# Phases before exponentials, and W1 by three powers: reordering the kernel-generation groups of an S4D block

## The chip, the cores and the metric

The kernel runs on one core of a Trainium2 chip. The metric is the device time of one execution in microseconds (us). The engines of a core run side by side, each with its own instruction queue worked off in order: PE (matrix products; its weight loads are listed as PEld), DVE (vector), ACT (activation functions and copies), POOL (vector work and DMA issue), SP (DMA issue). Semaphores order them.

## The reference

One transformer-like block over 2048 tokens of width 576, all in fp32: an S4D long convolution and a feed-forward layer, each behind a layer norm with scale and shift, and with a gated residual.

```python
# S4D: a long convolution per channel d, N = 128 complex states
A = -exp(log_A_real) + 1j * A_imag;  dt = exp(log_dt);  C = (C_real + 1j * C_imag) * dt
P = exp((A * dt)[:, :, None] * pos)              # pos = 0 .. 2047
K = 2 * einsum("dn,dnl->dl", C, P).real
y = irfft(rfft(u, 4096) * rfft(K, 4096))[:2048] + u * D_skip
# the block
sa, ca, ga, sb, cb, gb = split(silu(c) @ w_mod, 6)
h = layernorm(x) * (1 + ca) + sa
x = x + ga * S4D(h)
h = layernorm(x) * (1 + cb) + sb
x = x + gb * (relu(h @ w1) @ w2)                 # 576 -> 4608 -> 576
```

## The kernel before

**Stages.** The tokens are four blocks of 512. First the convolution kernel `K` is generated for block 0 of positions, in six groups of 96 channels (`KGen.first`, L324). Then block 0 is convolved (`Body.conv(0)`, L937) by short Fourier transforms on PE with butterflies on DVE, and normed. From there the feed-forward layer (`ffn`, L1264) runs over 4 x 36 steps, with fp32 split in a high and a low part, so 14 products a half step. Its steps are interleaved with the rest of the kernel values (`KGen.rest`) and the convolutions of blocks 1 to 3.

**One kernel group.** Position l is written as 16 coarse values of step 32 (`W1`) times 32 fine ones (`W2`); PE multiplies them over the 128 states (`products`, 96 pairs of small products for each half `u` of a group), and ACT copies the result to `ke` (`rows`, L351), which is stored to DRAM (`kd`) after every third group, and later loaded as `kt`. For each group:

- `turns` (L192): PE spreads the phases into PSUM (`ph`), ACT rounds them to an integer (`k`), DVE takes the difference (`f`, the phase within a turn). Three pieces: odd, even, powers.
- `exps` (L182): PE spreads the rates into PSUM (`ph`), ACT takes the exponential (`E`). Five pieces, E0 to E4.
- `sines` (L333): ACT takes sines and cosines of `f`, DVE and POOL multiply them by `E` into `W2`; `powers` (L262) makes the powers z^32 to z^1024 of which four stay in PSUM (`Z`), two are stored (`zs`, `Zd`); `moduli` multiplies the four by `E`.
- `doubling` (L283): `W1` grows from 1 value to 2, 4, 8, 16, each time by one power of `Z`: two products into `t` and `T`, and a difference and a sum. The first two take both halves of the group at once, the last two half by half; the last has its differences and sums on POOL.

In iteration g the loop finishes `W1` of group g, makes `E` and `f` of group g+1, copies `ke` of group g-1, then multiplies group g (first half `a` at once, second half `late` in portions in the next iteration, by `some`) and takes the sines of g+1.

**What sets the order.** All of `KGen` issues through helpers (`act` L58, `v` L61, `stt` L64, `pool` L67, `matmul` L70) that keep each engine's instructions in the order in which the program issues them. So the order written in `first` (L324) is the order on each queue. In the profile these helpers' lines stand for all instructions of `KGen`. `Kept` (L41, L47 in the profile) does the same elsewhere. The PSUM tiles of phases, rates and sines share one pair of buffers, taken in turn:

```python
def banks(self, name):
    return self.ph.tile([P, 2, 512], F32, tag="ph", bufs=2, name=name)
```

`ph` takes half of PSUM; `Z` (two banks), `T` and the result `kps` take the other half.

**Beside the groups.** `setup` (L82) prepares phases and rates of all channels, in portions; `mod` and `mod_late` (L736) make the modulation vectors; `early` (L607) loads x's first block, takes its statistics with the groups and makes `h`, in portions that the loop draws. `skip` adds `D_skip` to the first row of a loaded `kt`. In `conv(0)`, `spec_U` and `spec_K` make the spectra of x and `K` (`Ud`, `Rd` in DRAM, from POOL's queue).

## Time and profile before

| | |
|---|---|
| median of 3 runs | 1326.09 us (1322.65 to 1332.2) |
| profiled execution, its time and span | 1328.0 us, 1326.2 us |
| mean granted PE clock | 0.943 |
| busy in the span: PE, DVE, ACT, POOL | 1212.6, 895.2, 494.3, 160.3 us |
| kernel groups | about 35 to 160 us |
| first feed-forward product | 223.56 us |

How to read the rows that follow: a row of the timeline begins with the start and the duration in us, then the engine, the line in the kernel, the operation, the tiles written and read, and the shape. Instructions of a kind that follow one another are merged into a row (x4), whose duration runs from the first to the last. In brackets stands how long the engine was idle before, and what ended that ("issue": nothing that the profile shows). ACT, DVE and PE are the engines themselves, SPq and POOLq their DMA issues. On the page, part 2 cuts the span into 40 slices, with the busy share in tenths and the PE clock that the throttle granted in tenths of full speed.

### The profile page before, as it was taken

To read this page: it belongs to the slowest core of one execution; us is meant where nothing else is said; L and a number is where in the kernel's file an instruction comes from. 1 tells how busy PE (TensorE), PEld (TensorE's weight loads), DVE (VectorE), ACT (ScalarE), POOL (GpSimd) and SP (SyncE) were. 2 spreads that over 40 slices of the span, in tenths; PEclk is the share of its full clock that TensorE was granted. 3 is DMA by queue.
4 is the path that set the end of the run, shared out by engine and by line. 5 is a ranking of instruction groups with operands and counts; after the bars stand their busy time and mean duration, and the time that the engine had idled before them with its cause. 6 is when DMAs were issued, how large, how long until landed. Compare 5 with 4: busy or idle time off the path is not lost.

```text
span 1326.2 us, 25994 instructions
## 1 busy us (share of the span) xinstructions
PE 1212.6 (91%) x10720; PEld 960.7 (72%) x10720; DVE 895.2 (67%) x1324; ACT 494.3 (37%) x863; POOL 160.3 (12%) x256
## 2 busy tenths in 40 slices
PE   4566676899989999999999999999999999999998
PEld 3344554677767787777777887887888888888886
DVE  5989988999986999689468994457996222111112
ACT  5677623222223422622243225433323353223231
POOL 0756511011000100100001000100000000000000
PEclk9556777999989999999999999999999999999999
DMA  8567882889878967799779995867996667666652
GB/s 273 210 235 294 300 314 80 345 298 333 311 259 302 342 223 278 247 403 343 262 270 339 351 340 159 285 205 285 346 395 189 173 177 230 195 202 191 200 178 70
DMA packets 122635, 345.85 MB, mean 261 GB/s; under 512 B 23916, under 2 KB 24212, under 8 KB 111764
## 3 DMA queue, kind: packets, MB, share of 16 engines
q1 hardware_dynamic: 105940, 228.14, 51.8%
q0 software_dynamic: 16064, 114.67, 23.0%
q8 instruction: 84, 1.38, 0.4%
q10 hardware_dynamic: 512, 1.38, 0.3%
q14 instruction: 35, 0.29, 0.1%
HBM read 262.73 MB, written 81.40 MB: 259 GB/s over the span
## 4 chain that ended last, share of the span: by engine, by line
PE 70%; DVE 17%; DMA 6%; issue 4%; ACT 2%; POOL 1%; SPq 0%; ACTq 0%; DVEq 0%; POOLq 0%
PE hps L1330 28%; PE acc L1356 28%; PE ps_f L850 5%; DMA L1d<-w 3%; PE kps L71 2%; PE ph L71 2%; DVE W1r L484 2%; DVE T L482 2%; PE ps_i L1057 2%; PE kps L517 1%; DVE w L1300 1%; DMA x<-in_x_dram 1%; DVE W1r L486 1%; DVE W1r L488 1%; DVE w L1312 1%
## 5 line engine op out<-in xcount | busy, mean ns | idle before, releaser
L1330 PE MATMUL hps<-xh,w 128*128 128x512 f32 x1152 | 395.7, 404 | 0.7 <-ACT xh L47 0.7
L1356 PE MATMUL acc<-w,hh 128*128 128x512 f32 x1136 | 362.1, 401 | 3.7 <-ACT hh L1335 3.5
L1336 DVE SCALAR_TENSOR_TENSOR hl<-hps,hh 128x512 fp32r<-128x512 f32 x144 | 99.4, 690 | 309.2 <-ACT hh L1335 308.5
L1330 PEld LDWEIGHTS hps<-xh,w 128*128 128x128 f32 x1152 | 219.0, 191 | 48.9 <-ACT xh L47 1.3
L1356 PEld LDWEIGHTS acc<-w,hh 128*128 128x128 f32 x1136 | 212.4, 188 | 50.3 <-ACT hh L1335 4.4
L1330 PE MATMUL hps<-xl,w 128*128 128x512 f32 x576 | 228.0, 397 | 0.1
L1356 PE MATMUL acc<-w,hl 128*128 128x512 f32 x568 | 219.8, 399 | 1.5 <-DVE hl L1336 1.5
L1335 ACT ACTIVATE hh<-hps 128x512 fp32r<-128x512 f32 x144 | 86.0, 597 | 329.9 <-PE hps L1330 325.2
L1305 ACT ACTIVATE w<-r 128x576 fp32r<-128x576 f32 x141 | 96.7, 686 | 225.3 <-PE acc L1356 224.9
L1330 PEld LDWEIGHTS hps<-xl,w 128*128 128x128 f32 x576 | 109.2, 190 | 23.5 <-DVE xl L47 0.6
L1356 PEld LDWEIGHTS acc<-w,hl 128*128 128x128 f32 x568 | 106.1, 188 | 25.4 <-DVE hl L1336 3.3
L1295 ACT ACTIVATE w<-r 128x640 fp32r<-128x640 f32 x140 | 102.5, 732 | 51.2 <-DMA L1d<-w 50.5
L1330 PE MATMUL hps<-xs,w 128*128 128x512 f32 x288 | 98.7, 412 | 0.0
L71 PE MATMUL kps<-W,W 128*32 128x16 f32 x2304 | 39.4, 210 | 45.8 <-POOL W L68 28.1
L1036 DVE TENSOR_TENSOR Y<-Y,T 128x1152 f32<-128x1152 f32 x60 | 79.5, 1353 | 0.0
L71 PEld LDWEIGHTS kps<-W,W 128*32 128x32 f32 x2304 | 34.6, 142 | 59.5 <-POOL W L68 31.2
L851 ACT ACTIVATE Z<-ps_f 128x288 f32<-128x288 f32 x120 | 48.9, 409 | 71.1 <-PE ps_f L850 69.3
L517 PEld LDWEIGHTS kps<-W1r,W2r 128*32 128x32 f32 x3456 | 45.1, 113 | 38.6 <-issue 19.2
L517 PE MATMUL kps<-W1r,W2r 128*32 128x48 f32 (+2 forms) x3456 | 52.4, 202 | 15.5 <-ACT ker L527 10.8
L1330 PEld LDWEIGHTS hps<-xs,w 128*128 128x128 f32 x288 | 53.8, 190 | 11.3
L1356 PE MATMUL acc<-hh,w 128*128 128x512 f32 x142 | 56.9, 401 | 0.0
L1356 PE MATMUL acc<-hl,w 128*128 128x512 f32 x142 | 56.1, 395 | 0.0
(249 smaller groups left out, 1547.1 us busy)
## 6 DMA issues: line engine op xcount, KB each, us to landing
r<-in_w_dram SPq DMA_DIRECT2D x144, 320.0 KB, 6.0
r<-in_w_dram SPq DMA_DIRECT2D x144, 288.0 KB, 3.7
w<-L1d SPq DMA_DIRECT2D x108, 320.0 KB, 4.2
w<-L2d SPq DMA_DIRECT2D x108, 288.0 KB, 2.6
W2r<-W2d POOLq DMA_DIRECT2D x18, 1536.0 KB, 9.0
W2d<-W SPq DMA_DIRECT2D x12, 1536.0 KB, 8.7
Ua<-Ud POOLq DMA_DIRECT2D x15, 1152.0 KB, 9.3
W<-W1d POOLq DMA_DIRECT2D x18, 768.0 KB, 9.5
```

The source lines that it names most:

```text
L71: self.tc.keep_in_program_order(self.nc.tensor.matmul(*args, **kw))
L482: v(T, X, zi, op=ALU.mult)
L517: nc.tensor.matmul(ps[32 * dd : 32 * dd + 32, q, :], W2[:, r, ch], W1[:, r, ch], start=(r == 0), stop=(r == 1),)
L850: nc.tensor.matmul(o, fc[:, n2, c, :], src(n2), start=True, stop=True)
L851: ev = nc.scalar.activation(Z[:, n2, c], ps[:, :PC], AF.Copy)
L1036: v(y, y, T, op=op or ALU.add)
L1295: copy(g - 1)(w1[g][:, 0], r1[g], AF.Copy)
L1305: copy(g)(w[:, 0:D], r2[g], AF.Copy)
L1330: nc.tensor.matmul(ps, a, x, start=(i == 0), stop=(i == 13))
L1335: nc.scalar.activation(hh, ps, AF.Relu)
L1336: nc.vector.scalar_tensor_tensor(hl, ps, 0.0, hh, op0=ALU.max, op1=ALU.subtract)
L1356: nc.tensor.matmul(acc[i], a, x, start=(f == 0 and seen[i] == 1), stop=(f == NF - 1 and seen[i] == (3 if i < 4 else 2)),)
```

## The change

- *Order in a group.* The phases of the next group (`turns`) are issued ahead of its exponentials, in portions between the first two doublings; the five exponentials come after the first half of the new wide products. The statistics of x's tiles come after all of these.
- *W1 by three powers.* A seventh power, z^384, is made. The doublings for 8 and 16 values go. Instead `quarters` multiplies the first 4 values by z^128, z^256 and z^384 at once: for the real and for the imaginary part two products on DVE (96 x 3 x 4 = 1152 elements each) and one sum on POOL. `Z` holds five powers.
- *D_skip* is added by POOL to `ke` before it is stored, no longer to `kt` (`skip` goes); its array is laid out on the host as an added input layout.
- *x's spectra* of block 0, and that of `K`, are stored after the transform of the second `kt` has been issued, all three from POOL's queue in program order.
- *First phases early.* `setup` has one more portion: the phases of channels past the first third are prepared ahead of the silu of `c`, the rates after it.
- *mod_late* transposes each row one portion later; `zs` has a layout in which each half is stored contiguously.

```diff
@@ -32,7 +32,8 @@
 TURN_LO = 1.0 / TWO_PI - TURN_HI
-POWERS = (32, 64, 128, 256, 512, 1024)
+POWERS = (32, 64, 128, 256, 384, 512, 1024)
+NP = len(POWERS) - 2
 SLOTS = (*range(1, 32, 2), *range(0, 32, 2), *POWERS)
@@ -139,6 +140,7 @@
             turn(h)
+        yield
         self.act(lar[:, 4:], lar[:, 4:], AF.Exp)
@@ -182,7 +184,7 @@
         E = self.E[g] = []
-        for s0, n in ((0, 8), (8, 8), (16, 8), (24, 8), (32, 6)):
+        for s0, n in ((0, 8), (8, 8), (16, 8), (24, 8), (32, NS - 32)):
             e = self.pt.tile([P, 2, 8 * H], F32, tag="E", bufs=8, name=f"E_{g}")
@@ -192,7 +194,7 @@
         F = self.F[g] = []
-        for s0, n in ((0, 8), (17, 8), (32, 6)):
+        for s0, n in ((0, 8), (17, 8), (32, NS - 32)):
             k = self.pt.tile([P, 2, 8 * H], I32, tag="k", bufs=3, name=f"k_{g}")
@@ -261,50 +263,63 @@
-        Z = self.ps.tile([P, 2, 512], F32, tag="Z", name=f"Zp_{g}")[:, :, 0 : 4 * G]
+        Z = self.ps.tile([P, 2, 512], F32, tag="Z", name=f"Zp_{g}")[:, :, 0 : NP * G]
         Z = Z.rearrange("p r (i c) -> p r i c", c=G)
-        zs = self.pc.tile([P, 2, 2, G], F32, tag="zs", bufs=2, name=f"zs_{g}")
+        zs = self.pc.tile([P, 2, 2, 2, H], F32, tag="zs", bufs=2, name=f"zs_{g}")
         by_u = lambda x: x.rearrange("p i (u c) -> p u i c", u=2)
         c = self.abs(f)
-        self.act(by_u(Z[:, 1]), f[:, :, 0:4], AF.Sin, scale=-TWO_PI)
-        self.act(by_u(zs[:, :, 1]), f[:, :, 4:6], AF.Sin, scale=-TWO_PI)
-        self.cos(by_u(Z[:, 0]), c[:, :, 0:4])
-        self.cos(by_u(zs[:, :, 0]), c[:, :, 4:6])
+        self.act(by_u(Z[:, 1]), f[:, :, 0:NP], AF.Sin, scale=-TWO_PI)
+        self.act(zs[:, :, :, 1], f[:, :, NP:], AF.Sin, scale=-TWO_PI)
+        self.cos(by_u(Z[:, 0]), c[:, :, 0:NP])
+        self.cos(zs[:, :, :, 0], c[:, :, NP:])
         for r in (1, 0):
-            self.pool(by_u(zs[:, :, r]), by_u(zs[:, :, r]), e[:, :, 4:6], op=ALU.mult)
+            self.pool(zs[:, :, :, r], zs[:, :, :, r], e[:, :, NP:], op=ALU.mult)
         self.Z[g] = Z, zs
...
             for r in (1, 0):
-                self.v(by_u(Z[:, r]), by_u(Z[:, r]), e[:, :, 0:4], ALU.mult)
+                self.v(by_u(Z[:, r]), by_u(Z[:, r]), e[:, :, 0:NP], ALU.mult)
...
-    def doubling(self, g, i, u):
-
-        v, p = self.v, self.pool
-        Z = self.Z[g][0]
-        m, n = 1 << i, (u.stop - u.start) * H
-        W1 = self.W1[g][:, :, u].rearrange("p r u c a -> p r (u c) a")
+    def doubling(self, g, i):
+
+        v = self.v
+        m = 1 << i
+        W1 = self.W1[g].rearrange("p r u c a -> p r (u c) a")
         X, out = W1[:, :, :, 0:m], W1[:, :, :, m : 2 * m]
         zr, zi = (
-            Z[:, r, i, u.start * H : u.stop * H].unsqueeze(1).unsqueeze(3)
-            .broadcast_to([P, 2, n, m])
+            self.Z[g][0][:, r, i].unsqueeze(1).unsqueeze(3).broadcast_to([P, 2, G, m])
             for r in range(2)
         )
-        if m == 8:
-            t = self.pc.tile([P, 16 * H], F32, tag="T0", bufs=2, name="T0")
-            T = self.pc.tile([P, 16 * H], F32, tag="T1", bufs=2, name="T1")
-        else:
-            t = self.pc.tile([P, 8 * H], F32, tag="t", bufs=2, name="t")[:, : 2 * n * m]
-            T = self.ps.tile([P, 512], F32, tag="T", name="T")[:, : 2 * n * m]
-        t, T = (x.rearrange("p (r c a) -> p r c a", r=2, c=n) for x in (t, T))
+        t = self.pc.tile([P, 4 * G], F32, tag="t", bufs=2, name="t")[:, : 2 * G * m]
+        T = self.ps.tile([P, 512], F32, tag="T", name="T")[:, : 2 * G * m]
+        t, T = (x.rearrange("p (r c a) -> p r c a", r=2, c=G) for x in (t, T))
         v(t, X, zr, ALU.mult)
         v(T, X, zi, ALU.mult)
-        yield
-        add = p if m == 8 else v
-        add(out[:, 0], t[:, 0], T[:, 1], op=ALU.subtract)
-        add(out[:, 1], t[:, 1], T[:, 0], op=ALU.add)
+        v(out[:, 0], t[:, 0], T[:, 1], ALU.subtract)
+        v(out[:, 1], t[:, 1], T[:, 0], ALU.add)
+
+    def quarters(self, g):
+
+        v, p = self.v, self.pool
+        W1 = self.W1[g].rearrange("p r u c a -> p r (u c) a")
+        shape = [P, G, 3, 4]
+        X = [W1[:, r, :, 0:4].unsqueeze(2).broadcast_to(shape) for r in range(2)]
+        out = [W1[:, r, :, 4:16].rearrange("p c (j a) -> p c j a", j=3) for r in range(2)]
+        zr, zi = (
+            self.Z[g][0][:, r, 2:NP].rearrange("p j c -> p c j").unsqueeze(3).broadcast_to(shape)
+            for r in range(2)
+        )
+        for r, op in ((0, ALU.subtract), (1, ALU.add)):
+            T = self.pc.tile([P, 12 * G], F32, tag="T0", bufs=2, name="T0")
+            T = T.rearrange("p (c j a) -> p c j a", j=3, a=4)
+            v(out[r], X[r], zr, ALU.mult)
+            if r:
+                yield
+            v(T, X[1 - r], zi, ALU.mult)
+            p(out[r], out[r], T, op=op)
+            yield
@@ -346,12 +361,13 @@
             for u in range(2):
-                nc.sync.dma_start(out=k.Zd[2 * g + u], in_=zs[:, :, :, u * H : u * H + H])
+                nc.sync.dma_start(out=k.Zd[2 * g + u], in_=zs[:, u].rearrange("p i r c -> p (i r c)"))
...
             if g % 3 == 2:
+                self.pool(ke[:, 0], ke[:, 0], k.dsk[:, g // 3], op=ALU.add)
                 self.store(0, g // 3, ke.rearrange("p a q -> p (a q)"), nc.sync)
@@ -384,6 +400,7 @@
         run(turns, self.exps(0))
+        next(setup)
         next(mod)
@@ -394,38 +411,33 @@
             self.moduli()
-            if g + 1 == NG:
-                next(early)
-            double = [
-                self.doubling(g, i, u)
-                for i, u in (
-                    (0, slice(0, 2)), (1, slice(0, 2)), (2, slice(0, 1)), (2, slice(1, 2)),
-                    (3, slice(0, 1)), (3, slice(1, 2)),
-                )
-            ]
+            quarters = self.quarters(g)
             if g + 1 < NG:
+                turns = self.turns(g + 1)
+                next(turns)
+                some(late, 2)
+                self.doubling(g, 0)
+                next(turns)
+                some(late, 2)
+                self.doubling(g, 1)
+                next(mod, None)
+                next(turns)
+                next(quarters)
+                run(turns)
                 for i, _ in enumerate(self.exps(g + 1)):
                     some(late, 2 - i % 2)
-            run(*double[:2])
-            next(mod, None)
-            run(double[2])
-            if 0 < g < 5:
+                run(late, quarters)
+                if g > 0:
+                    next(early)
+            else:
                 next(early)
-            if g + 1 < NG:
-                turns = self.turns(g + 1)
-                for _ in range(2):
-                    next(turns)
-                    some(late, 2)
-                next(double[3])
-                next(turns)
-                run(late, turns, double[3])
-            else:
-                run(late, double[3])
-            if g + 1 == NG:
+                self.doubling(g, 0)
+                self.doubling(g, 1)
+                run(late)
                 next(early)
...
                 rows(g - 1)
-            run(*double[4:])
+            run(quarters)
             if g + 1 < NG:
@@ -594,8 +606,8 @@
             self.gb = self.sm.tile([P, D], F32, name="m_gb")
-            self.dsk = self.gb[0:1]
-            nc.gpsimd.dma_start(out=self.dsk, in_=I["dsk"].unsqueeze(0))
+            self.dsk = self.sm.tile([P, 2, 72], F32, name="dsk")
+            nc.gpsimd.dma_start(out=self.dsk, in_=I["dsk"])
             self.x2p = [self.pool(ctx, "x2a")]
@@ -636,7 +648,6 @@
         self.kt0 = kg.kt0
-        kept(self.skip(self.kt0, 0, nc.vector))
         for i in (0, 2, 1, 3):
@@ -739,26 +750,28 @@
             self.mod_weights(self.wm[nm], slice(j * D, (j + 1) * D), nc.sync)
+        yield
+        rows = {}
         for nm in ("sb", "cb", "gb"):
-            yield
-            w = self.wm[nm]
             ps = self.cps.tile([P, 512], F32, tag="cps", bufs=self.nps, name=f"mps_{nm}")
-            self.mod_products(ps, cb, w, nc.tensor.matmul)
-            row = self.cv.tile([P, 2 * P], F32, tag="row", bufs=1, name=f"row_{nm}")
+            self.mod_products(ps, cb, self.wm[nm], nc.tensor.matmul)
+            row = rows[nm] = self.cv.tile([P, 2 * P], F32, tag="row", bufs=2, name=f"row_{nm}")
             act(row[:, 0:P], ps[:, 0:P], AF.Copy)
...
                 act(row[0:32, o : o + 64], ps[0:32, P : P + 64], AF.Copy)
-            if nm == "gb":
-                yield
-                self.mod_spread(row, self.md[nm], self.m[nm], Kept(self.tc, nc.gpsimd))
-                return
-            ps = self.cps.tile([P, 512], F32, tag="cps", bufs=self.nps, name=f"mpt_{nm}")
-            nc.tensor.transpose(ps[:, 0:P], row[:, 0:P], self.ident)
-            nc.tensor.transpose(ps[:, P : P + 32], row[0:32, P:], self.ident[:32, :32])
-            act(
-                self.m[nm], ps[:, 0 : 5 * 32].rearrange("p (j r) -> p j r", r=32)[:, :, 0],
-                AF.Copy, bias=1.0 if nm == "cb" else 0.0,
-            )
+            nm = {"cb": "sb", "gb": "cb"}.get(nm)
+            if nm:
+                row = rows[nm]
+                ps = self.cps.tile([P, 512], F32, tag="cps", bufs=self.nps, name=f"mpt_{nm}")
+                nc.tensor.transpose(ps[:, 0:P], row[:, 0:P], self.ident)
+                nc.tensor.transpose(ps[:, P : P + 32], row[0:32, P:], self.ident[:32, :32])
+                act(
+                    self.m[nm], ps[:, 0 : 5 * 32].rearrange("p (j r) -> p j r", r=32)[:, :, 0],
+                    AF.Copy, bias=1.0 if nm == "cb" else 0.0,
+                )
+            yield
+        self.mod_spread(rows["gb"], self.md["gb"], self.m["gb"], Kept(self.tc, nc.gpsimd))
+        yield
@@ -969,8 +982,6 @@
             ktv = kt[p].rearrange("p (t dd g) q -> p t dd g q", t=2, g=2)
-            if s == 0 and p == 1:
-                self.skip(kt[p], p, Kept(self.tc, nc.gpsimd))
             src = lambda n2: ktv[:, n2 // 2, :, n2 % 2]
@@ -980,7 +991,7 @@
             yield -1
-            if s + 1 < NB or p == 1:
+            if s and (s + 1 < NB or p == 1):
                 self.save(self.Ud[s][p], U)
@@ -1088,7 +1099,8 @@
             yield from mm_K(1, ZK)
-            self.save(self.Rd[0][0], Ks[0], Kept(self.tc, nc.gpsimd))
+            for dst, t in zip((*self.Ud[0], self.Rd[0][0]), (*Us, Ks[0])):
+                self.save(dst, t, Kept(self.tc, nc.gpsimd))
         else:
@@ -1255,11 +1267,6 @@
-    def skip(self, kt, p, eng):
-        k0 = kt.rearrange("p (t dd g) q -> p t dd g q", t=2, g=2)[0:1, 0, :, 0]
-        dv = self.dsk.rearrange("o (dd p q) -> o dd p q", dd=4, p=2)[:, :, p]
-        return eng.tensor_tensor(k0, k0, dv, op=ALU.add)
-
     def ffn(self, gens):
@@ -1588,7 +1595,9 @@
     r["lv"] = np.array(SLOTS, dtype=np.float32)
-    r["dsk"] = a["A_D_skip"]
+    r["dsk"] = np.zeros((4, 32, 2, 72), np.float32)
+    r["dsk"][:, 0] = a["A_D_skip"][perm].reshape(2, 6, 4, 12).transpose(2, 0, 1, 3).reshape(4, 2, 72)
+    r["dsk"] = r["dsk"].reshape(P, 2, 72)
     w1 = a["B_w1"]
...
     r["w1"] = np.ascontiguousarray(w1.reshape(5, P, NF, P).transpose(2, 1, 0, 3))
```

## The prediction

> **What bounds the kernel now.** I read the page first: the slices, the clock and the chain of waits.
>
> ```profile
> span 1326.2 us, 25994 instructions
> DVE  5989988999986999689468994457996222111112
> PEclk9556777999989999999999999999999999999999
> PE 70%; DVE 17%; DMA 6%; issue 4%; ACT 2%; POOL 1%; SPq 0%; ACTq 0%; DVEq 0%; POOLq 0%
> ```
>
> A slice is 33 us. From about 230 us on, PE's feed-forward products carry the chain, and the change touches none of them. What it edits is the first six slices, where DVE looks full and PE's clock is at 0.5 to 0.7. A shift of the moment at which that part ends goes through to the end nearly one for one. So the question is what sets the pace of a kernel group, and the timeline answers it. Here is the group step that makes group 2 ready (start, duration, engine):
>
> ```profile
> 50.09 0.81 ACT L59 ACTIVATE s<-k 128x768 f32<-128x768 f32 x1
> 56.08 0.56 ACT L59 ACTIVATE Zp<-c,halfpi 128x384 f32<-128x384 f32 x1
> 57.04 1.28 ACT L59 ACT_TABLE_LOAD   x1
> 57.70 1.21 DVE L62 TENSOR_TENSOR Zp<-Zp,E 128x384 f32<-128x384 f32 x2
> 58.94 0.48 DVE L62 TENSOR_TENSOR t<-W,Zp 128x192 f32<-128x192 f32 x1
> 59.48 1.01 PE L71 MATMUL ph<-dl,zr 112*128 112x384 f32 x2
> 60.37 0.55 DVE L62 TENSOR_TENSOR t<-W,Zp 128x384 f32<-128x384 f32 x1
> 60.78 1.01 PE L71 MATMUL ph<-dl,zr 112*128 112x384 f32 x2
> 62.09 0.56 DVE L62 TENSOR_TENSOR t<-W,Zp 128x384 f32<-128x384 f32 x1
> 63.62 0.85 PE L71 MATMUL ph<-dp,zr 112*128 112x288 f32 x2
> 64.56 0.65 ACT L59 ACTIVATE E<-ph 128x576 f32<-128x576 f32 x1 [0.34 <-DVE st L623]
> 66.88 0.96 DVE L62 TENSOR_TENSOR k<-ph,k 128x768 f32<-128x768 f32 x1 [2.15 <-ACT k L59]
> 68.68 1.76 DVE L62 TENSOR_TENSOR k<-ph,k 128x768 f32<-128x768 f32 x2
> 69.56 0.48 ACT L59 ACTIVATE ke<-kps 128x384 f32<-128x384 f32 x1
> 70.06 1.28 ACT L59 ACT_TABLE_LOAD   x1
> 70.89 3.54 DVE L62 TENSOR_TENSOR T<-W,Zp 128x768 f32<-128x768 f32 x4
> 71.35 0.81 ACT L59 ACTIVATE s<-k 128x768 f32<-128x768 f32 x1
> ...
> 131.13 0.81 ACT L59 ACTIVATE s<-k 128x768 f32<-128x768 f32 x1
> ```
>
> I mark a group by its first sine on ACT (S). S of group 1 is 50.09, of group 2 71.35, of group 5 131.13: one step is 21.26 us, the four together 81.04. Within a step ACT is at sines until 57.04 (S+6.9), then table load, five exponentials fed by PE, three rounded phases, the copy of `ke`, a second table load, and the next S. DVE is not the pacemaker: it stands 2.15 us before the first `f`, waiting for ACT's `k`. It looks full because it runs some 3 us behind ACT. The pace is the ACT-PE chain, and the change has to be judged on that.
>
> **The group step after the change.** The order on ACT becomes sines, three `k`, five `E`, `ke`, sines; on DVE moduli, doubling 0, `f0`, doubling 1, `f1`, two wide products, `f2`, two wide products. `ph` has two buffers, taken in turn, and a phase product needs the buffer that was filled two before. Before, each `E` followed a buffer freed by ACT alone. Now E1's buffer is that of phase 2, which DVE frees only with `f2`, and `f2` stands behind two wide products. That such a wait is real shows already in group 1, where the third phase product waits for `f0`:
>
> ```profile
> 47.18 0.85 PE L71 MATMUL ph<-dp,zt 112*128 112x288 f32 x2 [1.00 <-DVE k L62]
> ```
>
> Two prices come from elsewhere: a wide product (1152 elements), and PE's phase products at full clock, where their pitch is shorter.
>
> ```profile
> 101.81 0.62 PE L71 MATMUL ph<-dl,zr 112*128 112x384 f32 x2 [0.25 <-ACT E L59]
> 103.59 0.53 PE L71 MATMUL ph<-dp,zr 112*128 112x288 f32 x2
> ...
> 175.26 2.62 DVE L47 TENSOR_TENSOR Y<-K,U 128x1152 f32<-128x1152 f32 x2
> ```
>
> A wide product: two in 2.62 less the overlap, so 1.27 each. From the 768-wide `T` row (3.54 for four, 0.87 each) in proportion 1.3: the bounds lie close together, I take 1.27. The walk from S:
>
> 1. The cosine for `Zp` ends at 56.64 = S+6.55 now; five powers instead of four widen it and the sine ahead of it by about 0.1 each: S+6.75. The second modulus needs it. The pair takes 58.94 - 57.70 = 1.24 now, a quarter wider about 1.45; the larger half of it lies behind the cosine: S+7.7 (7.5 to 7.9).
> 2. Doubling 0 is 60.37 - 58.94 = 1.43, `f0` 0.88 (half of 1.76), doubling 1 62.09 - 60.37 = 1.72, `f1` 0.88, two wide products 2.54, `f2` 0.9 (seven powers for six): S+16.05. The three `k` are ready when DVE wants them (ACT free from S+6.9, their phases ready), so DVE does not stand here.
> 3. PE starts E1's product there. Now E1 starts at 59.48 and E4 at 63.62, 4.14 with the same share of late products in between; E4's exponential starts 0.94 after its product and takes 0.65, a sixth wider 0.73: S+21.85.
> 4. `ke` to table load 0.50, table load to S 1.29: next S at S+23.65.
>
> So a step takes 23.65 where 21.26 was measured at the same half clock: the first table load, 1.28, is now hidden in the wait for E0, but ACT stands for `f2`. At full clock E2 to E4 is 1.78 instead of 2.84; E1 to E4 shrinks in that ratio to 2.6 and the last half step by 0.3: 21.8. Which clock? The rows show both in this stage, 1.01 at 60.78 and 0.62 at 101.81; the page's slices are mostly at 0.5, and the change leaves PE only one pair of products between phase 2 and E1. So I take half clock for all four steps: 4 x 23.65 - 81.04 = +13.6; at full clock throughout it is +6.2. The Trainium skill ("TensorE: Matmul & The Clock Gate", Part 1: The HAM clock gate) would leave only the first: the clock rises after some 3.4 us of sustained work and falls again after idling. No row here shows that length by itself.
>
> The DVE work saved (below) and the gaps of PE lie beside this chain. POOL gets two wide adds for four narrow ones:
>
> ```profile
> 64.18 1.15 POOL L68 TENSOR_TENSOR zs<-zs,E 128x192 f32<-128x192 f32 x2
> 72.78 3.90 POOL L68 TENSOR_TENSOR W<-T,T 128x384 f32<-128x384 f32 x4 [7.17 <-DVE T L62]
> ```
>
> 192 elements cost 0.58, 384 cost 0.98, so 1152 about 2.6. The last ends some 2.6 after the last wide product, near S+21.2; group products follow on PE beside the sines and delay nothing.
>
> **The start.**
>
> ```profile
> 22.51 0.17 DVE L679 TENSOR_SCALAR ex<-ex 128x5 f32<-128x5 f32 x1 [4.84 <-ACT ex L59]
> ...
> 34.86 0.36 DVE L62 TENSOR_TENSOR Tc<-cc,s 128x192 f32<-128x192 f32 x1
> ...
> 39.74 1.19 DVE L62 TENSOR_TENSOR Zp<-Zp,E 128x384 f32<-128x384 f32 x2
> ```
>
> The phases of the other groups now run in the 4.84 us that DVE stands idle; group 0's moduli come at 34.9 instead of 39.74 (at least 0 if the rows land late, at most 4.84 saved). From 34.9 the same walk, without late products: 1.45 + 1.43 + 0.88 + 1.72 + 0.88 + 2.54 + 0.9 to the end of `f2` at 44.7, four products at 1.01 and the last exponential to 49.5, table load: S of group 1 at 50.8, against 50.09. The new chain eats the gain: +0.7. S of group 5 moves by +0.7 + 13.6 = +14.3.
>
> **The last group and the first convolution.**
>
> ```profile
> 140.91 0.48 DVE L62 TENSOR_TENSOR t<-W,Zp 128x192 f32<-128x192 f32 x1
> 147.63 0.74 DVE L641 TENSOR_TENSOR h<-h,m_ca 128x576 f32<-128x576 f32 x1
> 153.46 3.54 DVE L62 TENSOR_TENSOR T<-W,Zp 128x768 f32<-128x768 f32 x4
> 161.84 1.73 PEld L71 LDWEIGHTS kps<-W,W 128*32 128x32 f32 x174 [0.39 <-issue]
> 176.11 0.49 ACT L59 ACTIVATE ke<-kps 128x384 f32<-128x384 f32 x1 [13.75 <-PE kps L71]
> 185.64 1.01 POOL L47 TENSOR_TENSOR kt<-kt,m_gb 1x288 f32<-1x288 f32 x1 [14.95 <-DMA kt<-kd]
> 194.24 2.90 DVE L47 TENSOR_TENSOR K<-Z 128x576 f32<-128x576 f32 x6 [3.97 <-ACT Z L892]
> ```
>
> Relative to S of group 5, doubling 0 keeps its place (it follows ACT's square root, after the sines). The third doubling goes: doubling 1 ends at 144.06 by the row, `h` (5.83, from 147.63 to 153.46) is done 3.6 earlier, and with it x's transforms and the group's products (161.84). Four wide products instead of four `T` leave DVE 1.9 earlier. The chain then runs products, `ke`, store, load of `kt`, its transform, and DVE's K at 194.24, where DVE stood 3.97; so K can come at most 1.9 + 3.97 = 5.9 earlier. Terms: -3.6; the skip add on POOL (1.01) leaves the chain, a 128x72 add before the store enters (0.2 to 0.6, below the 192-wide row): -0.6. Then the spectra:
>
> ```profile
> Ud<-U POOLq DMA_DIRECT2D x7, 1152.0 KB, 8.0
> ...
> PE kps L71 <- issue: 14.1, 4, 5.4
> ```
>
> PE's group products stand 14.1 us in four gaps where nothing but the instruction stream can be late, while x's two spectra and the weights cross the DMA engines. Without the spectra I take 2.5 back (0 to 5). The Trainium skill ("Runtime: NRT & Kernel Launch", Instruction fetch mechanics) says that each engine's queue fetches the next block of 256 instructions while one is worked off, at a cost mostly hidden. By that this term would be 0 and the time 2.5 longer; the trace, with 14.1 us of such gaps, speaks against it. But the three saves are now on POOL with nothing before them but the new add: the `kt` add that held up the third is gone. They are issued as `kd` is stored and `kt` loaded, 3.4 MB beside that chain; a lone one takes 8.0. I take 3.7 (0 to 8). Sum of the tail: -3.6 - 0.6 - 2.5 + 3.7 = -3.0 (-5.9 to +3.8). The pipelined modulation rows and the contiguous `Zd` stores lie on PE and SP beside waits for `kt`: nothing; if that cover went, a few tenths. All others of the changed queues (SP's `W1d`) have their old place behind POOL's add.
>
> Sum: +14.3 - 3.0 = +11.3. The profiled execution took 1328.0 (span 1326.2 and 1.8 around it), 1.9 above the median 1326.09. It would become 1339.3; on the median, 1337.
>
> **Rivals.**
> - *DVE is the bound after all.* For: its slices at 9. Two halves of the third doubling (3.4, as wide as doubling 1) and `T` (3.5) go, 5.1 + 0.2 come: -1.6 for each of five steps, -8; with the start, -4.8, and DVE's tail, -1.9, this gives -14.7: 1311. It decides if a step falls below 21.26, that is if E1 to E4 do not follow `f2`. Against: the 2.15 us stand. 0.13.
> - *Same chain, PE at full clock in the exponentials.* +0.7 + 6.2 - 3.0 = +3.9: 1330. For: the four steps average 20.26, below the 21.26 of the one at half clock, so the clock was up in some. 0.17.
> - *The saves are not later where it matters.* They take the DMA from `kd` and `kt` for the whole 8 and the gaps stay: +14.3 + 3.8 = +18.1: 1344. 0.2.
> - The forecast, 1337: 0.5.
>
> **Numbers.** About 1%, 13 us, is what a measurement tells from no change. The forecast, 1337, lies inside, below the upper bound of 1339, and its tail's bounds reach from 1334 to 1344; the third rival lies beyond, the first just beyond 1313 on the other side. Slower: 0.17 of the third and 0.1 of the forecast's 0.5, 0.27. Faster: 0.1 of the first. Within 1%: 0.63. Range 1318 to 1345: it leaves out the first rival and what lies above the third.
>
> **What would show it.** S to S near 23.65 in the new timeline; E1's product (`ph<-dl,zr`) waiting for DVE `k`; DVE idle before the next `Tc` by 4 to 5 us, while before it ran behind; the gaps of `kps` after x's transforms shorter; the three saves of spectra issued right behind POOL's new add, and `kt` landing late. Wrong if E1 does not wait, or if the steps are at or below 20 us.

## The result, and the profile after

The changed kernel takes 1343.3 us in the median of six runs (1340.84 to 1346.87), beside 1325.82 for the kernel before on the same chip (1322.65 to 1332.2): a ratio of 1.0128, 95% interval 1.0099 to 1.0156. It is slower by 1.3%, 17 us. The forecast of 1337 was 6 us too low, and the result lies inside its range; of the three classes, "slower by over 1%" had 0.27.

The page of the changed kernel, the four lines that answer to those shown of before:

```profile
span 1343.0 us, 25931 instructions
DVE  7878877899995899769757986457997222111112
PEclk9555768899998999999999999999999999999999
PE 62%; DVE 15%; DMA 7%; issue 2%; POOL 1%; ACT 1%; SPq 1%; DVEq 0%; ACTq 0%; POOLq 0%
```

The span is 16.8 us longer, and DVE is less busy in the first slices (7 and 8 where it was 8 and 9, the very first apart): the change removed work from an engine that is not full. In a step its busy time falls from 18.4 us on average to 17.1. The first feed-forward product starts at 241.68 instead of 223.56, 18.1 us later; 1.3 us of that comes back before the end. So the whole loss lies ahead of that point, and it splits into two halves at S of group 5, the last first sine. The timeline of one step of the changed kernel, from S of group 2 to S of group 3, and S of group 5:

```profile
72.89 0.81 ACT L60 ACTIVATE s<-k 128x768 f32<-128x768 f32 x1
73.74 0.36 DVE L63 TENSOR_TENSOR Tc<-cc,s 128x192 f32<-128x192 f32 x1 [3.68 <-ACT s L60]
84.82 0.95 DVE L63 TENSOR_TENSOR k<-ph,k 128x768 f32<-128x768 f32 x1
85.69 1.34 DVE L63 TENSOR_TENSOR W<-W,Zp 128x1152 f32<-128x1152 f32 x1
85.82 1.01 PE L72 MATMUL ph<-dl,zr 112*128 112x384 f32 x2 [1.52 <-DVE k L63]
86.95 1.35 DVE L63 TENSOR_TENSOR T<-W,Zp 128x1152 f32<-128x1152 f32 x1
87.73 1.01 PE L72 MATMUL ph<-dl,zr 112*128 112x384 f32 x2 [0.31 <-ACT E L60]
88.21 0.85 DVE L63 TENSOR_TENSOR k<-ph,k 128x672 f32<-128x672 f32 x1
88.67 0.44 PE L72 MATMUL kps<-W,W 128*32 128x16 f32 x16
89.12 1.01 PE L72 MATMUL ph<-dl,zr 112*128 112x384 f32 x2
95.39 0.81 ACT L60 ACTIVATE s<-k 128x768 f32<-128x768 f32 x1
...
140.39 0.81 ACT L60 ACTIVATE s<-k 128x768 f32<-128x768 f32 x1
```

A step is 22.50 us, where the four steps before took 20.26 on average. DVE now stands 3.68 us at the head of each step, waiting for ACT's sine, so DVE is not full; but a stretch of it now lies on the chain. E0's product (85.82) waits for `f1`, which ends at 85.77 and stands on DVE behind the moduli, `f0` and two doublings. From there the five exponentials, by PE and ACT in turn, lead to the next S. `f2` (the `k<-ph,k` of 672 elements) costs little: while it holds its buffer, E1's product (87.73) waits 0.31 us for E0's exponential, and E2's product, at 89.12, does follow the end of `f2` at 89.06, but PE is busy with group products until 89.11 in any case.

The granted clock is 0.50 in all four steps. In the kernel before it is 0.50, 0.50, 0.69 and 0.59, for steps of 21.26, 21.35, 18.42 and 20.01 us. So of the 8.96 us that the four steps lose, some 4.8 (1.2 a step) stand against steps at the same clock, and some 4.2 against two steps of a higher one; what raised the clock there, the rows do not show. S of group 5 is 140.39 against 131.13, +9.26 us.

The other half, +8.98 us, lies behind it, on the path of the last kernel rows to the second transform:

```profile
116.78 0.33 POOL L69 TENSOR_TENSOR ke<-ke,dsk 128x72 f32<-128x72 f32 x1
...
167.65 2.02 PE L72 MATMUL kps<-W,W 128*32 128x16 f32 x172 [1.65 <-POOL W L69]
178.62 1.31 PE L72 MATMUL kps<-W,W 128*32 128x16 f32 x81 [1.78 <-issue]
180.02 0.49 ACT L60 ACTIVATE ke<-kps 128x384 f32<-128x384 f32 x1 [13.73 <-PE kps L72]
180.58 6.75 POOL L69 TENSOR_TENSOR ke<-ke,dsk 128x72 f32<-128x72 f32 x1 [12.99 <-ACT ke L60]
183.25 2.62 DVE L48 TENSOR_TENSOR Y<-K,U 128x1152 f32<-128x1152 f32 x2
185.79 1.35 DVE L48 TENSOR_TENSOR T<-K,U 128x1152 f32<-128x1152 f32 x1
187.17 1.38 DVE L48 TENSOR_TENSOR Y<-Y,T 128x1152 f32<-128x1152 f32 x1
187.28 1.11 POOL L48 DMA_DIRECT2D Ud<-U  x2
187.36 1.11 SPq L462 DMA_DIRECT2D kd<-ke  x2
188.38 0.53 POOL L48 DMA_DIRECT2D Rd<-K  x1
195.42 0.37 SPq L1265 DMA_DIRECT2D kt<-kd  x1
202.26 1.30 PE L902 MATMUL ps_f<-kt,fcK 128*128 128x288 f32 x2 [13.35 <-DMA kt<-kd]
212.48 2.90 DVE L48 TENSOR_TENSOR K<-Z 128x576 f32<-128x576 f32 x6 [5.63 <-ACT Z L905]
```

The new add of the skip values takes 0.33 us for the first half of the channels and 6.75 us for the second, both 128x72. The store of `ke` waits for it, and the three stores of spectra leave POOL's queue beside that store (from 187.28 on). Of before, the rows of the same path that the prediction did not need:

```profile
174.72 1.31 PE L71 MATMUL kps<-W,W 128*32 128x16 f32 x81 [3.70 <-issue]
176.63 1.11 SPq L450 DMA_DIRECT2D kd<-ke  x2
179.74 0.37 SPq L1253 DMA_DIRECT2D kt<-kd  x1
186.71 0.75 PE L889 MATMUL ps_f<-kt,fcK 128*128 128x288 f32 x2 [0.25 <-POOL kt L47]
```

Each link of this path, before and after (all from the rows of the two kernels, S of group 5 at 131.13 and 140.39):

| us | before | after | difference |
|---|---|---|---|
| S of group 5 to copy of `ke` | 44.98 | 39.63 | -5.35 |
| copy of `ke` to its store | 0.52 | 7.34 | +6.82 |
| store of `kd` to load of `kt` | 3.11 | 8.06 | +4.95 |
| load of `kt` to PE's transform | 6.97 | 6.84 | -0.13 |
| PE's transform to DVE's K | 7.53 | 10.22 | +2.69 |
| sum | 63.11 | 72.09 | +8.98 |

So the tail's own gain, 5.35 us, did arrive, and three new costs of 14.5 us together took it back. The gain has two parts. The last run of group products starts on PE 27.26 us behind S instead of 30.71 (167.65, two of its 174 products apart, and 161.84 before), and from there to the copy of `ke` it is 12.37 us instead of 14.27, of which 1.92 is the shorter last gap (1.78 and 3.70). These gaps of PE come at a fixed distance: the last two have 128 products and 128 weight loads between them, in both kernels.

### The profile page after: what moved, and what is told of

It reads as the page before. It is cut to its first block, busy times and chain, and to the rows that moved or that the text cites. A ratio compares the mean times of both kernels' runs of the same rounds, so it can differ in the third digit from the quotient of the medians.

```text
span 1343.0 us, 25931 instructions
## 1 busy us (share of the span) xinstructions
PE 1218.2 (91%) x10720; PEld 963.4 (72%) x10720; DVE 888.2 (66%) x1275; ACT 496.5 (37%) x863; POOL 175.2 (13%) x245
## 4 chain that ended last, share of the span: by engine, by line
PE 62%; DVE 15%; DMA 7%; issue 2%; POOL 1%; ACT 1%; SPq 1%; DVEq 0%; ACTq 0%; POOLq 0%
PE hps L1337 27%; PE acc L1363 27%; PE ps_f L863 4%; DMA L1d<-w 3%; DVE T L494 2%; DVE W1r L496 2%; PE ps_i L1068 2%; PE kps L529 1%; DVE w L1307 1%; DMA x<-in_x_dram 1%; DVE W1r L498 1%; DVE w L1319 1%; DVE W1r L500 1%; DVE Y L1047 1%; DMA Ua<-Ud 1%
## 5 line engine op out<-in xcount | busy, mean ns | idle before, releaser
L1337 PEld LDWEIGHTS hps<-xs,w 128*128 128x128 f32 x288 | 53.6, 189 | 11.3
```

The costliest lines, as they stand in the source:

```text
L1337: nc.tensor.matmul(ps, a, x, start=(i == 0), stop=(i == 13))
```

## The experiments

The kernel before ran beside each set; its medians there were 1327.3, 1328.4 and 1327.1 us, so ratios are what is compared. A kernel's profile is one execution, and its span scatters by some us between executions; from the profiles I read places ahead of 240 us, not totals.

### The third phase ahead of the wide products

```diff
@@ changed kernel, first()
-                next(quarters)
                 run(turns)
+                next(quarters)
```

> The changed kernel with one line moved: the third difference, `f2`, ahead of the first two wide products on DVE; everything else as changed. Theory: a group step is 22.5 us because the third exponential's product on PE waits for `f2`, which stands behind two wide products. Then the exponentials' products follow one another from S+12.9 on and a step becomes 21.3 to 21.5 (S to S); four and a half steps at -1.1: about -5, 1338 us against 1343. Rival: the step is long because ACT takes the rounded phases ahead of the exponentials at all, whatever `f2` does: step 22.5 as before, 1343.

Measured 1340.16 us, ratio 1.0094 (1.0065 to 1.0123), not separable in time from the changed kernel. The step was a miss: 22.05 us (S at 114.58 and 136.63), neither 21.4 nor 22.50. Its timeline:

```profile
104.46 1.72 DVE L63 TENSOR_TENSOR k<-ph,k 128x768 f32<-128x768 f32 x2
105.47 1.01 PE L72 MATMUL ph<-dl,zr 112*128 112x384 f32 x2 [1.53 <-DVE k L63]
114.58 0.82 ACT L60 ACTIVATE s<-k 128x768 f32<-128x768 f32 x1
```

`f2` no longer holds a buffer when E1 needs one: E1's product follows PE's other products at once, 1.53 us behind E0's instead of 1.91. That is most of the 0.45 us that a step gains. The rest of the step is as before: E0's product stands 12.93 us behind S in both kernels, since it waits for `f1`, which stands behind the two doublings on DVE. From E0's product on, five exponentials at PE's half-clock pace of 1.4 us lead to S 9.1 us later.

### The skip value back on the loaded rows

The new add on `ke` goes, and `skip` on `kt` is as in the kernel before; all else stays. With it POOL waits for `kt` before it issues the three stores.

```diff
@@ changed kernel, rows() and conv()
-                self.pool(ke[:, 0], ke[:, 0], k.dsk[:, g // 3], op=ALU.add)
+        kept(self.skip(self.kt0, 0, nc.vector))
+            if s == 0 and p == 1:
+                self.skip(kt[p], p, Kept(self.tc, nc.gpsimd))
```

> The changed kernel with the D_skip part alone undone: added to the loaded `kt` as in the kernel before (DVE for the first, POOL for the second), not to `ke`. This also puts the three saves of spectra behind POOL's wait for `kt`. Theory: POOL's add to `ke` (6.75 us, where the same add took 0.33 in an earlier group) is held up by DVE's run of operations with two SBUF inputs, and the three saves slow the store of `kd` (issue of the store to issue of the load 8.06 us against 3.11). Both go: `ke` to store 0.5, store to load 3.1, and POOL's add of 1.0 comes back: about -10.5, 1332 to 1333. Rival: the add is not on the path, since the weights' loads or PE hold the second transform anyway: 1341 to 1343.

Measured 1330.81 us, ratio 1.002 (0.9997 to 1.0044): 14 us of the 17 go with this one edit (1.0128 less 1.002, of 1326), which takes away the add and also the collision of the stores; the next run parts the two. Copy to store is 0.52 us again, store to load 3.12, PE's transform to K 7.54; the first feed-forward product comes 88.64 us behind S of group 5 (101.29 in the changed kernel, 92.43 before). Its cost shows on DVE:

```profile
180.39 1.11 SPq L461 DMA_DIRECT2D kd<-ke  x2
183.51 0.37 SPq L1267 DMA_DIRECT2D kt<-kd  x1
189.52 0.75 PE L902 MATMUL ps_f<-kt,fcK 128*128 128x288 f32 x2 [1.23 <-POOL kt L48]
202.75 1.36 DVE L48 TENSOR_TENSOR Y<-K,U 128x1152 f32<-128x1152 f32 x1 [2.80 <-DMA Rd<-K]
```

The product Y is written over the buffer that the late store of K still reads, and waits 2.80 us.

### The add kept, the three stores held back

The changed kernel with a small copy on POOL that reads the loaded `kt`, ahead of the three stores.

```diff
@@ changed kernel, conv()
+            gate = self.sm.tile([P, 72], F32, name="gate")
+            Kept(self.tc, nc.gpsimd).tensor_copy(gate, kt[1][:, 0])
             for dst, t in zip((*self.Ud[0], self.Rd[0][0]), (*Us, Ks[0])):
```

> The changed kernel with one small POOL copy that reads the loaded second `kt`, put ahead of the three saves of spectra in POOL's queue, so that they start only when `kt` is there; POOL's add to `ke` stays. It separates the two causes of the tail. Theory: the add still stands some 6.5 us, but store to load falls from 8.06 to about 3.1 and the load is not slower: -5, 1338. Rival: the saves do not slow the store, whose packets are simply late: 1343. If the saves were the whole of it: 1332.

Measured 1340.44 us, ratio 1.0091 (1.006 to 1.0123). Store to load is 3.12 us again and load to transform 4.59 instead of 6.84: the stores' collision is undone, worth 7.2 us at that point. The add is not: 7.01 us.

```profile
179.40 7.01 POOL L69 TENSOR_TENSOR ke<-ke,dsk 128x72 f32<-128x72 f32 x1 [12.74 <-ACT ke L60]
194.14 1.30 PE L902 MATMUL ps_f<-kt,fcK 128*128 128x288 f32 x2 [7.46 <-DMA kt<-kd]
211.13 1.36 DVE L48 TENSOR_TENSOR Y<-K,U 128x1152 f32<-128x1152 f32 x1 [4.10 <-DMA Rd<-K]
```

The first feed-forward product moved by only 3.1 us behind S (98.17, 101.29), since 4.1 us turn into Y's wait for the store of K, now later; in time the intervals of this kernel and of the changed one overlap. Between this kernel and the one before it in this list stand 0.7%, 9 us, and 9.5 us at the first feed-forward product (98.17 and 88.64 behind S): the price of the add, with the half clock behind it (below).

### x's spectra stored as before

The kernel with the skip value on the loaded rows, and x's spectra stored where they were; what is left of the change is the group order, W1 by three powers and the early phases.

```diff
@@ conv()
-            if s and (s + 1 < NB or p == 1):
+            if s + 1 < NB or p == 1:
...
-            for dst, t in zip((*self.Ud[0], self.Rd[0][0]), (*Us, Ks[0])):
-                self.save(dst, t, Kept(self.tc, nc.gpsimd))
+            self.save(self.Rd[0][0], Ks[0], Kept(self.tc, nc.gpsimd))
```

> The changed kernel with D_skip undone as in the run e2_skipkt, and in addition the spectra of x saved where the kernel before saved them, right after each is made. What is left of the change is the group order, the start and the small parts. It prices the later saves by themselves, against e2_skipkt. Theory: with the saves early the gaps of PE's group products (9.1 us in the profile before, 7.0 after) come back to about 9, and the result is 2 us slower than e2_skipkt: 1334 to 1335. Rival: the later saves bring nothing: the same as e2_skipkt within 1 us.

Measured 1333.33 us, ratio 1.0043 (1.0023 to 1.0062): the group part of the change alone loses some 6 us. The copy of `ke` comes 41.85 us behind S of group 5, 2.3 later than with the late stores (39.57), as the 2.5 of the prediction said; but Y does not wait here, and the first feed-forward product stands at 88.55 behind S, as with them (88.64). So in this pair the late stores gain 2.3 us at one place and pay them back at the next. The medians differ by 2.5 us the way that the expectation had it, but the intervals overlap. The 2.3 us lie in PE's last gap ahead of `ke`, 3.97 us here and 1.50 with the late stores. That the stores cause it is not shown: in the next run, which has the stores of the kernel before, this gap is 1.78.

### The early phases alone

```diff
@@ kernel before, setup() and first()
+        yield
         self.act(lar[:, 4:], lar[:, 4:], AF.Exp)
...
         run(turns, self.exps(0))
         next(setup)
+        next(mod)
+        next(setup)
-        next(mod)
-        next(setup)
```

> The kernel before with one part of the change alone: the first phases ahead of the two exponentials in the set-up. Theory: in the changed kernel the first moduli stood 4.1 us earlier (35.67 against 39.74) and the new order of the group step took the gain back before the second group's first sine; in the old order the gain stays, so this kernel has its second group's first sine at some 46 to 47 instead of 50.09 and takes some 1322 to 1324. Rival: the second group's first sine is set by something else that does not move (x's front, the PE), it stands near 50 and the time is that of before, 1326 to 1327.

Measured 1321.15 us, ratio 0.9956 (0.9929 to 0.9984). S of group 1 is at 45.37 instead of 50.09, even a little earlier than expected, and S of group 5 at 127.58, 3.55 earlier. How this reaches the end is not clear from its profile:

```profile
173.14 0.49 ACT L59 ACTIVATE ke<-kps 128x384 f32<-128x384 f32 x1 [11.01 <-PE kps L71]
173.66 1.27 SPq L452 DMA_DIRECT2D kd<-ke  x2
177.98 0.37 SPq L1255 DMA_DIRECT2D kt<-kd  x1
```

`ke` is 2.97 us earlier, but its store now follows x's second spectrum by 3.3 us instead of 6.5 and takes 4.32 to the load; the first feed-forward product is only 0.72 earlier (222.84). The rest of that execution's gain lies in the feed-forward part, where its first 200 us had a granted clock of 0.99 against 0.96 in the profiled execution of before. Whether the early start causes that stays open.

### The add as a probe in the kernel before

An add of the same size on POOL, from `ke` and a constant tile into a tile that nobody reads, behind the last copy of `ke`.

```diff
@@ kernel before, rows()
+            if g == 5:
+                self.pool(k.probe[:, 0], k.probe[:, 1], ke[:, 0], op=ALU.add)
```

> The kernel before with one more instruction off the path: POOL adds the first 72 columns of the last rows ke to a constant tile and writes a tile that nobody reads, right behind ACT's copy of these rows; the store does not wait for it. Theory: the 6.75 us of the add in the changed kernel are starvation by the DVE instructions beside it, whose inputs lie both in SBUF; the same DVE run follows the copy in the kernel before, so this add, too, takes several us (over 2) instead of the 0.33 us that the same shape took where DVE waited, and the time stays that of before within 3 us. Rival: the 6.75 us come from something in the changed kernel alone (the write back into ke, the saves behind it); then this add takes 0.2 to 0.6 us.

```profile
177.93 3.08 POOL L68 TENSOR_TENSOR probe<-probe,ke 128x72 f32<-128x72 f32 x1 [11.04 <-ACT ke L59]
179.46 1.34 DVE L47 TENSOR_TENSOR T<-K,U 128x1152 f32<-128x1152 f32 x1
180.84 1.38 DVE L47 TENSOR_TENSOR Y<-Y,T 128x1152 f32<-128x1152 f32 x1
180.95 0.57 POOL L845 DMA_DIRECT2D Ud<-U  x1
190.54 1.33 PE L893 MATMUL ps_f<-kt,fcK 128*128 128x288 f32 x2 [3.44 <-POOL kt L47]
```

The probe takes 3.08 us in a kernel that has none of the change: the add is slow because of what runs beside it, not because of the rest of the change. It starts 1.0 us into the pair of products Y, and ends 0.2 us after the end of the first `T` (180.80), which is where the add ended in the changed kernel (187.33 against 187.14), in the kernel with the held stores (186.41, 186.21) and in that with the third phase first (183.55, 183.35). The expectation of an unchanged time is not borne out: its one run took 1333.07 us, beside a median of 1328.41, which by itself decides nothing (the runs of before reach from 1320.92 to 1337.86), but the first feed-forward product comes at 230.21, 97.57 behind S instead of 92.43. I had overlooked POOL's queue: the store of x's second spectrum stands behind the probe, leaves at 180.95, meets the load of `kt`, and the transform starts 9.6 us after the load's issue (180.98) instead of 7.0.

### All phases first

The kernel with the skip value on the loaded rows, and with all three phases ahead of the wide products, two of them ahead of the first doubling.

```diff
@@ first()
                 next(turns)
                 some(late, 2)
-                self.doubling(g, 0)
                 next(turns)
                 some(late, 2)
+                next(turns)
+                self.doubling(g, 0)
+                run(turns)
                 self.doubling(g, 1)
                 next(mod, None)
-                next(turns)
                 next(quarters)
-                run(turns)
```

> The changed kernel with all three rounded phases ahead of the wide products (two ahead of the first doubling, the third ahead of the second) and with the skip value added on POOL to the loaded rows again, as in the kernel before. Theory: with the phases ahead only the conversion of phases to sines and the exponentials are left in a step; the step falls from 22.50 to 19.5 to 20.6 us, under the 20.26 of before on average, the last first-sine stands near 130, the tail is that of the kernel with the skip value on the loaded rows (first ffn product 88.6 us behind it against 92.4 before), and the time is 1317 to 1322, faster than both kernels. Rival: the step stays at the 22.05 that the run with the third phase ahead of the first wide product showed, since the exponentials go at the half clock's pace of PE; then the time is 1328 to 1331.

Measured 1322.27 us, ratio 0.9949 (0.9924 to 0.9973). S stands at 46.13, 68.62, 89.61, 109.18 and 128.75: the last two steps are 19.57 at a granted clock of 0.59 and the first two 22.49 and 20.99 at 0.50, so the four average 20.66, no better than the 20.26 of before. Step and time lie just above what was expected (19.5 to 20.6, and 1317 to 1322), and the rival's 22.05 fell. The kernel is 4.0 us ahead at S of group 1, by the early start, and 2.4 at S of group 5. The first feed-forward product is 92.78 behind S, not 88.6: the copy of `ke` comes 3.1 us later behind S than in the kernel with the changed phase order and the skip value on the loaded rows (42.71, 39.57), and Y's wait for the store of K is 1.0 longer. The 3.1 us arise ahead of the transform of x, which starts on PE 3.4 us later behind S (23.22, 19.81); the gap of PE before the last group products ahead of it is 5.06 us instead of 1.50. Why that gap is longer, the rows do not show.

```profile
195.27 1.36 DVE L48 TENSOR_TENSOR Y<-K,U 128x1152 f32<-128x1152 f32 x1 [3.78 <-DMA Rd<-K]
```

### The add on DVE

```diff
@@ changed kernel, rows()
-                self.pool(ke[:, 0], ke[:, 0], k.dsk[:, g // 3], op=ALU.add)
+                self.v(ke[:, 0], ke[:, 0], k.dsk[:, g // 3], op=ALU.add)
```

> The changed kernel with the one add of the skip values to ke on DVE instead of POOL, in the same place of the program. Theory: the POOL add was slow because DVE's instructions kept it from SBUF, so on DVE itself it takes under 0.5 us and waits for at most one DVE instruction: copy of ke to store 0.7 to 2.5 us instead of 7.34, and the time falls by 5 us and by up to 5 more if the three saves, no longer behind the add, are through before the store: 1333 to 1338. Rival: the store was held by something else, or the saves cost as much wherever they go: 1342 to 1344.

```profile
180.79 0.23 DVE L63 TENSOR_TENSOR ke<-ke,dsk 128x72 f32<-128x72 f32 x1 [16.54 <-ACT ke L60]
181.05 1.12 SPq L462 DMA_DIRECT2D kd<-ke  x2
189.25 0.75 PE L902 MATMUL ps_f<-kt,fcK 128*128 128x288 f32 x2
210.27 2.89 DVE L48 TENSOR_TENSOR K<-Z 128x576 f32<-128x576 f32 x6
```

The add takes 0.23 us, copy to store is 0.79 us, and PE's transform starts 13 us earlier than in the changed kernel. Yet the time is 1341.93 us, ratio 1.01 (1.005 to 1.0151). DVE stood 16.54 us for `ke` with the whole of x's transforms queued behind the add, and K comes at 210.27 because DVE is late, not PE. Neither theory had this: an add moved to another engine takes its wait with it.

### Two orders of the stores

The kernel with all phases first, once with x's spectra stored as before, once with the store of K ahead of those of x:

```diff
@@ conv(), the second of the two
-            for dst, t in zip((*self.Ud[0], self.Rd[0][0]), (*Us, Ks[0])):
+            for dst, t in zip((self.Rd[0][0], *self.Ud[0]), (Ks[0], *Us)):
```

> The kernel with the phases first and the skip value on the loaded rows, with x's two spectra stored where the kernel before stored them (only the kernel's first spectrum is stored late, as there). Theory: the late stores pay back what they gain: with the late skip, first kernel rows copied 2.3 us later as between the two runs with and without late stores (41.85 against 39.57 behind the last first sine), but the product Y no longer waits 3.78 us for the store of the kernel's spectrum; the two cancel within 2 us of the kernel with the phases first, 1320 to 1324. Rival: the late stores are worth their 2.5 us here too, since Y's wait lies beside other work: 1324 to 1326.

> The kernel with the phases first and the skip value on the loaded rows, with the three late stores in the other order: the kernel's spectrum K first, x's two spectra behind it. Theory: the product Y is written into the buffer that the store of K still reads, and K's store stood third in the queue; as the first of the three it lands before Y, the wait of 3.78 us of Y for it falls under 0.5, and the time falls by 2 to 4 us, to 1318 to 1320. Rival: Y waits for the second kernel spectrum's store, issued 3.5 us before it, or for x's stores as much: no change, 1322 within 1.

Stored as before: 1319.05 us, ratio 0.9924 (0.9893 to 0.9955), a microsecond under what the theory of cancelling stores had. Only half of that theory is seen: Y no longer waits, and PE's last gap is longer (3.97 us, 1.51 with the late stores), but `ke` is copied no later behind S (42.14, 42.71), because the gap ahead of x's transform is 1.78 instead of 5.06. Late stores as they are bring nothing here either. K's store first: 1319.02 us, ratio 0.9939 (0.9911 to 0.9968), as its theory had it. In this one Y's wait falls from 3.78 to 0.35 us, and from K to the first feed-forward product it is 29.44 us instead of 32.94, though K itself now waits 1.86 us for the same store:

```profile
185.84 2.90 DVE L48 TENSOR_TENSOR K<-Z 128x576 f32<-128x576 f32 x6 [1.86 <-DMA Rd<-K]
189.09 1.36 DVE L48 TENSOR_TENSOR Y<-K,U 128x1152 f32<-128x1152 f32 x1 [0.35 <-DMA Ud<-U]
```

Both beat the kernel before and the changed one. The three kernels with all phases first and the one with the early start alone cannot be told apart by their intervals, so that the early start may be all of their gain.

## Why the prediction was right or wrong

The sum against what the two profiles show, up to the first feed-forward product:

| step of the prediction | predicted | measured |
|---|---|---|
| start: S of group 1 | +0.7 | +0.30 |
| four steps | +13.6 | +8.96 |
| third doubling: start of the last run of group products | -3.6 | -3.45 |
| gaps of PE: from there to the copy of `ke` | -2.5 | -1.90 |
| skip add | -0.6 | +6.82 (copy to store) |
| three stores beside `kd` and `kt` | +3.7 | +4.95 (store to load), -0.13 (load to PE) |
| PE's transform to K | not in the sum | +2.69 |
| K to first feed-forward product | 0 | -0.12 |
| sum | +11.3 | +18.12 |

- **The bound** was right. DVE's busy time in a step fell by 1.3 us (forecast 1.6), and the time rose; DVE waits 3.68 us for ACT in each step (forecast 4 to 5). The rival of a full DVE fell: a step is longer than 21.26, not shorter. But the chain is no longer one of ACT and PE alone: from the moduli to `f1` it goes through DVE, as the walk of the prediction had it.
- **The start** was right: moduli at 35.67 (forecast 34.9), and the new group order eats the gain by S of group 1. The run with the early phases alone shows that in the old order it stays.
- **The group step** had the walk on DVE right and the link to PE wrong. `f2` ends at S+16.17, forecast S+16.05. But E1 does not wait for it, and by the prediction's own sign ("Wrong if E1 does not wait") this step failed: "`ph` has two buffers, taken in turn" does not hold. E1's product follows E0's exponential (`[0.31 <-ACT E L60]` at 87.73), so it was given the buffer that E0 had freed, and `f2` kept the other. The wait for DVE that counts is E0's, for `f1`. From the end of `f2` to the next S it is 6.33 us, not 7.6: one product less lies there. That is 1.3 us a step, which less the 0.12 of `f2` makes up the row's difference of 4.6 us. The clock was forecast right: 0.50 in all four steps. The run with the third phase first shows how little hung on `f2`: 0.45 us a step.
- **The third doubling and the gaps** came out near their terms. That the gaps were due to x's spectra stays open, as shown above: the gap is short in one kernel with the early stores too. And of the "four gaps" of 14.1 us only two, 9.1 us, can stand beside x's spectra: the other two end at 140.71 and 144.16, ahead of their first store (164.67). The 128 products and 128 weight loads between two gaps are 256 instructions, the size of the block that the prediction names; that the gaps are late fetches would fit this, but no run shows it.
- **The skip add** was the step that failed worst: "a 128x72 add before the store enters (0.2 to 0.6, below the 192-wide row)". It was priced by its size from a row where DVE was not in the way; beside DVE's products it took 6.75. The bounds were both from the same kind of row, so no bound caught it. The probe shows that the add is slow by what runs beside it and not by the rest of the change, and its cost, 9.5 us at the first feed-forward product, is the difference of the two runs that both hold the stores back, one with it and one without.
- **The late stores** collide as forecast, at a higher price: 7.2 us by the run that held them back, inside the bounds of 0 to 8, but 3.7 was taken. In the table a part of it is hidden, since load to PE also lost the `kt` add of some 1.0 us. What the prediction did not have is their second cost: K's store still holds the buffer that Y is written to, 2.8 to 4.1 us in the runs where the stores come later still.
- **The half clock** of the transform was a term left out. In the changed kernel PE had stood 13.35 us for `kt`; its first pair of products took 1.30 us instead of 0.75, and the granted clock was 0.50 from 202.3 to 207.2 and 1.00 from 207.9 on, where before it was 1.00 throughout.
- **The number.** The rival whose 1344 us came nearest, stores that are not later where it matters, is not what happened: PE's gaps did shrink and the steps were 4.6 us cheaper than it assumed. The errors in the sum, -4.6 in the groups, +7.4 at the add, the 1.1 at the stores and the missing 2.7, partly hid each other. That 1343 lies inside the range is in part luck. "Within 1%" was the likeliest class, and the result is just beyond it.

## What to carry to other kernels

A small operation put on the path of a store costs what its engine lets it have at that moment: price it by a row from the same neighbourhood, not by its size, and look at what is queued behind it and what runs beside it. When transfers are moved later, ask which buffer they hold and which store or load they will meet. And where a wait hangs on one of two buffers, read from the trace or the order of instructions which of them the next user gets, rather than assume that they alternate.

## What the runs showed of the hardware

**POOL beside DVE.** The same 128x72 add took 0.33 us while DVE stood (116.78 in the changed kernel), and 3.08, 5.93, 6.75 and 7.01 us when it started in DVE's run of products with both inputs in SBUF. In all four it ended 0.2 us after the first `T`, where the next instruction, `Y<-Y,T`, starts only after `T` has ended (187.14 and 187.17 in the changed kernel), while the ones ahead of it overlap (`Y` ends at 185.87, `T` starts at 185.79). The Trainium skill ("SBUF — State Buffer", Who interferes with whom) says that a DVE instruction with two SBUF inputs contends with a GpSimd instruction that reads SBUF, over a port pair that is an exclusive lock. The trace agrees that POOL blocks, but here it was not for one instruction of 0.5 to 1.35 us: it went on through nine of them in the changed kernel (the six of K, two `Y` and `T`), until DVE itself paused. That the shared port is the reason is argued from that page and from these ends; no row names it.

**PE's clock after a wait.** The first pair of products of the transform took 0.75 us in every kernel where PE had stood at most 1.58 us just before (among them the kernel before, 0.25, and the skip value on the loaded rows, 1.23), and 1.30 to 1.33 us after 3.44, 7.46, 13.34 and 13.35 us (the probe, the held stores, the third phase first, the changed kernel). From PE's start to DVE's K it was 7.53 and 7.54 us in the first two named and 9.5 to 10.4 in these four. In the changed kernel the granted clock was 0.50 for the first 4.9 us of the transform and 1.00 behind them. The Trainium skill ("TensorE: Matmul & The Clock Gate", What's actually happening) puts the fall at one idle window of about 3.4 us; these rows agree with it, the 3.44 us of the probe barely. So a load that is late by more than that may cost PE 2.7 us on top (10.22 less 7.53).
